# Delta rule and soft mixture of slots on one core: the experts' products turned around and put side by side in the array

## The chip, the cores and the metric

The kernel runs on one core of a Trainium2 chip, in one launch. A core has five engines that work at the same time and wait for each other only through semaphores: TensorE (PE in the profile, with PEld for its loads of the stationary operand), VectorE (DVE), ScalarE (ACT), GpSimd (POOL) and SyncE (SP), which here issues most of the DMAs. The metric is the device time of one execution in microseconds, 921.85 as the median of three (921.1 to 922.2).

A matmul holds one operand still in the 128 x 128 array, at most 128 columns of it, and streams the other one, at most 512 columns here, past it. The result lies in PSUM with one partition for each column of the stationary operand. In float32 each matmul of the program is two MATMUL instructions in the trace, each with a load of its own; a transpose is one.

## The reference, cut to what matters

The first part is a gated delta rule over 768 tokens for 4 batch rows and 8 heads of 48. The change does not touch it. Its output, as x of 3072 tokens by 384, goes through a soft mixture with 8 experts of 4 slots each:

```python
logits = x @ phi                        # 3072 x 32
d = softmax of logits over the tokens   # a column sums to 1
slot_input = (d.T @ x).reshape(8, 4, 384)
for e in range(8):
    h = np.maximum(slot_input[e] @ w1[e], 0.0)    # 4 x 384 @ 384 x 1024
    slot_out[e] = h @ w2[e]                       # 4 x 1024 @ 1024 x 384
c = softmax of logits over the slots    # a row sums to 1
return c @ slot_out.reshape(32, 384)              # 3072 x 32 @ 32 x 384
```

Both w1[e] and w2[e] are 1.57 MB in float32, 25 MB for all experts.

## The kernel before

The first part runs in 24 chunks of 32 tokens, in six groups of four. Each group's logits and both softmaxes (`route`) run beside the next group's chunks, and the slots' sums over the tokens are kept as `sacc`, 96 partitions x 4 x 32: 384 input features (in four pieces `h` of 96) by 32 slots. The token weights over the slots stay in `Call`. The last group's routing has nothing beside it (L529).

The stage of the experts begins at L533, when the buffers of the first part are released (L530). The names that matter:

- `w1t`, `w2t`: an expert's weights on chip. Two w1 (experts 0 and 1) are loaded early in the first part (L499, pool `wpool`); the other 14 tiles, 6 of w1 and 8 of w2, are issued at L534 to L537 on SyncE's queue. A w1 is two DMAs of 48 partitions each, a w2 one DMA of 128 partitions. There are 4 buffers for the later w1 and 5 for w2, so the fifth w1 and the sixth w2 wait until an earlier one was read for the last time.
- L557, `first`: for an expert and each of eight pieces `t` of 128 hidden units, w1's piece (96 x 128) is loaded into the array and the expert's 4 slots stream past it, four times to add up the pieces `h`: 256 matmuls. The result `ph` has the hidden units on partitions, as the second product needs it.
- L561: relu on VectorE, into the expert's own 4 columns of `hx`, whose other columns are zero.
- L568, `second`: `hx` (128 x 32) stands in the array and 384 columns of w2 stream past it, 64 matmuls that all add into one `pso` of 32 partitions x 384.
- L577: 24 transposes make `cT` from `Call`, 32 slots on partitions.
- L582: `so` is `pso` over the softmax's sums. L588: 24 products `pout` of 128 tokens x 384, `cT` standing, `so` streaming, 32 rows deep. L591 and L593 copy each to `ob` on VectorE and ScalarE in turn; L594 stores it from SyncE's queue.

A tile framework orders the instructions of each engine: within its priorities and waits it may put steps of the stage in another order than the code. The order in which TensorE takes them is shown with the change.

Of the kernel before, what the change touches and what calls it, by code (L numbers as in the profile page):

```python
# [16 lines left out]
def kernel(  # L17
# [8 lines left out]
    moe_w2: bass.AP,  # L26
    out: bass.AP,
):
    """Gated delta rule in chunks of 32 tokens, then the slot mixture.

    A "unit" is four heads x 32 tokens of one batch row on the 128 partitions, u = (b, g) with
    head = 4 g + h, partition = 32 h + t.  In a chunk with the state S before it:
        (I + L) w = V - Kn S,   L[t, s] = beta_s kn_t.kn_s  (s < t),   u_s = beta_s w_s
        y = Q S + strict_lower(Q Kn^T) u,      S += Kn^T u
    The inverse of I + L comes from elimination by columns, one 32 x 32 block per partition, for
    four chunks (all their 128 blocks) at once; it doesn't depend on the state and runs ahead.
    The softmax over the tokens is kept online, chunk group by chunk group.
    """
    nc = tc.nc
    P = 128  # L40
    B, H, S, D = q.shape
# [23 lines left out]
    def pt(shape):  # L65
        return ps.tile(shape, F32, name="pt", tag="pt", bufs=2)

# [1 line left out]
    Ks = [io.tile([P, GC, U, DP], F32, name=f"Ks{i}", bufs=1) for i in range(2)]  # L69
    Qs = io.tile([P, GC, U, DP], F32, name="Qs", bufs=1)  # L70
    Vt = {}
# [23 lines left out]
    for i, tag in enumerate(("Lc", "lb", "tt")):  # L95
# [4 lines left out]
                in_=beta.rearrange("b (g h) (c t) -> h (b g) c t", h=4, t=C)[  # L100
                    h, :, i * NB:(i + 1) * NB])
        bts.append(t)
    # the same by blocks: partition 32 h + 8 c + u of a group of chunks
    bb = cpool.tile([P, NG, C], F32, name="bb")
    load_k(0)
    load_q(0, nc.scalar)
# [10 lines left out]
            out=phi[g * D:(g + 1) * D],  # L117
            in_=moe_phi[g * 4 * D:(g + 1) * 4 * D].rearrange("(h d) s -> d h s", h=4))

# [1 line left out]
    ident = cpool.tile([P, P], F32, name="ident")  # L121
    make_identity(nc, ident)
    hm = cpool.tile([P, 4], F32, name="hm")
# [31 lines left out]
        nc.vector.memset(t, 0.0)  # L155
        St.append(t)

# [1 line left out]
    NW1 = 2  # L159
    w1t, w2t = {}, {}  # L160

# [7 lines left out]
    def load_w2(e, pool, bufs):  # L169
        w2t[e] = pool.tile([P, NFC, Dm], F32, name="w2t", tag="w2t", bufs=bufs)  # L170
        nc.sync.dma_start(out=w2t[e], in_=moe_w2[e].rearrange("(t p) d -> p t d", p=P))

# [1 line left out]
    # Each of these gives a list of steps, which the chunks' chain is interleaved with.  # L174
    KQ, AT, KX, Lc, TTb = {}, {}, {}, {}, {}

    def norm(n):
        Kf = Ks[n % 2].rearrange("p c u d -> p (c u) d")
        ssq = small.tile([P, GC * U], F32, name="ssq", tag="ssq")
        nrm = small.tile([P, GC * U], F32, name="nrm", tag="nrm")  # L180
        rn = small.tile([P, GC * U], F32, name="rn", tag="rn")

        def squares():
            sq = wk.tile([P, GC * U, D], F32, name="sq", tag="KX")
            nc.gpsimd.tensor_tensor(sq, Kf[:, :, 0:D], Kf[:, :, 0:D], op=ALU.mult)
            nc.vector.tensor_reduce(ssq, sq, axis=AX.X, op=ALU.add)

        def root():
            # with a Newton step behind the table's value
            nc.vector.tensor_scalar(ssq, ssq, 1e-30, None, op0=ALU.max)  # L190
            nc.scalar.activation(nrm, ssq, ACT.Sqrt)
            nc.vector.reciprocal(rn, nrm)
            nc.vector.tensor_tensor(rn, rn, ssq, op=ALU.mult)
            nc.vector.tensor_tensor(nrm, nrm, rn, op=ALU.add)
            nc.vector.tensor_scalar(nrm, nrm, 0.5, 1e-6, op0=ALU.mult, op1=ALU.add)
            nc.vector.reciprocal(rn, nrm)

        def scale():
            nc.gpsimd.tensor_tensor(Kf[:, :, 0:D], Kf[:, :, 0:D],  # L199
                                    rn.unsqueeze(2).broadcast_to([P, GC * U, D]), op=ALU.mult)  # L200

        return [squares, root, scale]

    def prep(n, c):
        """Of a chunk: Kn and Q transposed, strict_lower(Q Kn^T) and Kn Kn^T (both transposed)."""
        cc = n * GC + c

        def transposes(bh):
# [29 lines left out]
                + [lambda g=g: products(g) for g in range(G)])  # L238

    def invert(n):  # L240
        """(I + L)^-1 transposed: tt[block][k][i] = T[i, k], a block on each partition."""
        st = {}

        def spread():
# [29 lines left out]
        return [spread] + [lambda j=j: eliminate(j) for j in range(C - 1)] + [store]  # L274

    def near(cc):
        """Of the next chunk: its inverse as weights, and Kn spread by heads."""
        n, c = divmod(cc, GC)

        def inverse():  # L280
            for h in range(4):
                nc.sync.dma_start(
                    out=TTs[cc % 2][C * h:C * h + C, :, h, :],
                    in_=TTb[n][C * h + c * U:C * h + (c + 1) * U].rearrange("u k i -> k u i"))

        def keys(g):
            if g == 0:
                KX[cc] = wk.tile([P, G, B, 4, D], F32, name="KX", tag="KX")
            kn = Ks[n % 2].rearrange("p c (b g) d -> p c g b d", g=G)[:, c, g, :, 0:D]
            for b in range(B):  # L290
                nc.gpsimd.tensor_tensor(  # L291
                    KX[cc][:, g, b], kn[:, b].unsqueeze(1).broadcast_to([P, 4, D]),
                    hm.unsqueeze(2).broadcast_to([P, 4, D]), op=ALU.mult)

        return [inverse] + ([lambda g=g: keys(g) for g in range(G)] if cc < NCH - 1 else [])

# [1 line left out]
    def chunk(cc, Yn, fill):  # L298
        n, c = divmod(cc, GC)
        kq, T, at = KQ.pop(cc), TTs[cc % 2], AT.pop(cc)  # L300
# [60 lines left out]
                                 start=False, stop=True, skip_group_check=True)  # L361
            nc.scalar.activation(Yn[:, c, :, g * D:(g + 1) * D], py, ACT.Copy)

# [1 line left out]
    Call = cpool.tile([P, NG, B, NSL], F32, name="Call")  # L365
    dsum = cpool.tile([P, NSL], F32, name="dsum")
    sacc = cpool.tile([GD, 4, NSL], F32, name="sacc")
# [3 lines left out]
    def route(n, Yn):  # L371
# [28 lines left out]
                                    op=ALU.mult)  # L400

        def maximum():
            # the running maximum over the tokens, on every partition
            cm = small.tile([P, NSL], F32, name="cm", tag="cm")
            nc.vector.tensor_reduce(cm, lg.rearrange("p b s -> p s b"), axis=AX.X, op=ALU.max)
            pm = pt([NSL, P])
# [30 lines left out]
                                    op=ALU.mult)  # L437

        def repeat():
            # the weights of 32 tokens, for each of the four heads of a unit  # L440
            pd = pt([P, GC, B, NSL])
            for c in range(GC):
                nc.tensor.matmul(pd[:, c].rearrange("p b s -> p (b s)"),
# [30 lines left out]
    NF = 5  # L474

    class Fill:
        """Some of the steps at each call, evenly over a chunk's NF calls."""

        def __init__(self, steps):
            self.steps, self.at, self.calls = steps, 0, 0  # L480
# [6 lines left out]
                self.steps[self.at - 1]()  # L487

    def merge(*lists):
        """The lists' steps, each list spread evenly over the whole."""  # L490
        keyed = [((i + 0.5) / len(ls), j, f) for j, ls in enumerate(lists) for i, f in enumerate(ls)]
        return [f for _, _, f in sorted(keyed, key=lambda x: x[:2])]

# [35 lines left out]
    drain(routing)  # L529
    att.close()  # L530

# [1 line left out]
    wp2 = ctx.enter_context(tc.tile_pool(name="wts2", bufs=1))  # L533
    for e in range(E):  # L534
        if e >= NW1:
            load_w1(e, wp2, 4)
        load_w2(e, wp2, 5)  # L537
    pd = pt([NSL, 1])
    nc.tensor.matmul(pd, lhsT=dsum, rhs=ones, start=True, stop=True)
    rd = cpool.tile([NSL, 1], F32, name="rd")  # L540
    nc.vector.tensor_scalar(rd, pd, 1e-9, None, op0=ALU.add)
    nc.vector.reciprocal(rd, rd)
    # each expert's slots in their own columns, the others' zero, so that all add up in one place
    hx = wp2.tile([P, E, NFC, NSL], F32, name="hx")
    nc.gpsimd.memset(hx, 0.0)
    pso = ps.tile([NSL, Dm], F32, name="pso", tag="psW")

    def first(e):
        """relu(slots w1), transposed: w1 is the stationary operand."""
        sl = slice(e * SPE, (e + 1) * SPE)  # L550
        st = {}

        def product(t):
            if t == 0:
                st["ph"] = ps.tile([P, NFC, SPE], F32, name="ph", tag="psR", bufs=2)
            for h in range(4):
                nc.tensor.matmul(st["ph"][:, t, :], lhsT=w1t[e][:, h, t * P:(t + 1) * P],  # L557
                                 rhs=sacc[:, h, sl], start=(h == 0), stop=(h == 3))

        def relu():  # L560
            nc.vector.tensor_scalar(hx[:, e, :, sl], st["ph"], 0.0, None, op0=ALU.max)  # L561

        return [lambda t=t: product(t) for t in range(NFC)] + [relu]

    def second(e):
        """w2 is the moving operand, so that its products pass beside the loads of w1."""
        def product(t):
            nc.tensor.matmul(pso, lhsT=hx[:, e, t, :], rhs=w2t[e][:, t, :],  # L568
                             start=(e == 0 and t == 0), stop=(e == E - 1 and t == NFC - 1))

        return [lambda t=t: product(t) for t in range(NFC)]

    cT = wp2.tile([NSL, NG, B, P], F32, name="cT")
    for n in range(NG):
        pc = pt([NSL, B, P])
        for b in range(B):
            nc.tensor.transpose(pc[:, b, :], Call[:, n, b, :], ident)  # L577
        nc.scalar.activation(cT[:, n], pc, ACT.Copy)
    for e in range(E + 1):
        drain(merge(*([second(e - 1)] if e else []), *([first(e)] if e < E else [])))  # L580
    so = cpool.tile([NSL, Dm], F32, name="so")
    nc.vector.tensor_scalar(so, pso, rd, None, op0=ALU.mult)  # L582

    for n in range(NG):
# [38 lines left out]
```

## Time and profile before

| | |
|---|---|
| median of three executions | 921.85 us |
| the profiled execution's span | 919.5 us |
| median less span | 2.35 us |
| span, mean granted clock of TensorE | 0.701 |
| first DMA of the experts' stage issued | at 736.57 us |
| sum `so` begins | at 887.87 us |
| last `pout` product ends | at 915.98 us |

The span runs from the first to the last instruction of the profiled execution. The profile gives each stretch's granted clock of TensorE as a share of 2.4 GHz: 0.50 is its lower level, 1.2 GHz, and 1.00 the upper one. Times in views of the trace count from the start of the span. A busy PE may be streaming, or loading the stationary operand between short streams; the two are told apart by PEld's time beside it.

### The profile page before, as it was taken

Reading aid. Unit: us, or ns where it says so; the run is one execution under the profiler, and the core shown is the slowest. Engines: PE = TensorE matmul, PEld = TensorE weight load, DVE = VectorE, ACT = ScalarE, POOL = GpSimd, SP = SyncE. Lnnn points to the kernel's source line nnn. Section 1 sums busy time; section 2 is a strip of 40 time slices with the busy share of each in tenths; the row PEclk is TensorE's granted clock in tenths of the full one; section 3 lists DMA queues with packets and bytes.
Section 4 is the critical chain, followed back from the end, with each engine's and each line's share of the span. In section 5 each row is a group of like instructions: output and inputs, shape, how many; then the busy total and the mean of one; then the engine's idle time right before and its main releaser. Section 6 shows DMA issues by size and latency. Waiting matters only on the chain.

```text
span 919.5 us, 19108 instructions
## 1 busy us (share of the span) xinstructions
PE 679.9 (74%) x8324; PEld 565.6 (62%) x8324; DVE 299.4 (33%) x816; ACT 101.3 (11%) x223; POOL 192.9 (21%) x347
## 2 busy tenths in 40 slices
PE   1706569069990799807998069996499799999998
PEld 1504569058880688706888058885398696765754
DVE  3267112942139421394213942226421100000011
ACT  0303000021120211102111021111000110000001
POOL 7231213131251213412134111351210200000000
PEclk9999999999995555755557555565555567667765
DMA  6240763023310242102321021000100099990013
GB/s 118 37 85 26 133 115 72 1 52 55 75 20 0 58 70 55 20 0 58 69 55 19 0 58 32 25 2 0 35 13 1 1 266 211 237 231 16 1 60 146
DMA packets 148019, 58.12 MB, mean 63 GB/s; under 512 B 131968, under 2 KB 143328, under 8 KB 147936
## 3 DMA queue, kind: packets, MB, share of 16 engines
q1 hardware_dynamic: 141888, 55.87, 27.9%
q10 hardware_dynamic: 5664, 0.94, 0.6%
q8 instruction: 65, 1.06, 0.5%
q0 software_dynamic: 384, 0.10, 0.1%
q14 instruction: 18, 0.15, 0.1%
HBM read 45.86 MB, written 11.01 MB: 62 GB/s over the span
## 4 chain that ended last, share of the span: by engine, by line
PE 64%; DVE 17%; DMA 6%; POOL 4%; SPq 3%; ACT 3%; issue 2%; ACTq 0%; DVEq 0%; POOLq 0%
PE ph L557 9%; PE psW L324 8%; PE psY L359 7%; DVE pr L264 7%; PE pso L568 6%; PE psS L340 6%; DVE tt L267 6%; PE pt L215 5%; PE pt L385 5%; PE pt L458 3%; PE pout L588 3%; PE psR L310 2%; PE pt L230 2%; PE psY L354 2%; PE pt L379 2%; SPq L77 2%
## 5 line engine op out<-in xcount | busy, mean ns | idle before, releaser
L215 PE MATMUL pt<-ident,Ks 128*128 128x128 f32 x96 | 42.1, 438 | 167.9 <-POOL Ks L199 158.7
L291 POOL TENSOR_TENSOR KX<-Ks,hm 128x192 f32<-128x192 f32 x184 | 91.0, 531 | 354.0 <-PE psS L340 264.4
L215 PEld LDWEIGHTS pt<-ident,Ks 128*128 128x128 f32 x96 | 20.8, 216 | 173.9 <-POOL Ks L199 159.6
L324 PE MATMUL psW<-R,TT 128*128 128x48 f32 x384 | 86.6, 396 | 34.4 <-DMA TT<-td 31.2
L324 PEld LDWEIGHTS psW<-R,TT 128*128 128x128 f32 x384 | 81.1, 311 | 39.4 <-DMA TT<-td 19.1
L557 PEld LDWEIGHTS ph<-sacc,w1t 96*128 96x128 f32 x512 | 87.8, 272 | 3.8 <-issue 3.8
L557 PE MATMUL ph<-sacc,w1t 96*128 96x4 f32 x512 | 88.1, 310 | 0.0
L359 PE MATMUL psY<-U,AT 128*128 128x48 f32 x384 | 83.9, 393 | 0.0
L264 DVE TENSOR_TENSOR pr<-tt,lb 128x31 f32<-128x31 f32 (+15 forms) x186 | 76.7, 413 | 16.2 <-POOL lb L252 11.0
L359 PEld LDWEIGHTS psY<-U,AT 128*128 128x128 f32 x384 | 78.2, 306 | 3.4
L267 DVE TENSOR_TENSOR tt<-tt,pr 128x31 f32<-128x31 f32 (+15 forms) x186 | 73.3, 394 | 5.2
L340 PE MATMUL psS<-U,KX 128*48 128x48 f32 x1472 | 69.8, 271 | 0.0
L340 PEld LDWEIGHTS psS<-U,KX 128*48 128x48 f32 x1472 | 60.8, 181 | 6.3 <-issue 1.7
L568 PE MATMUL pso<-w2t,hx 128*32 128x384 f32 x128 | 58.5, 627 | 1.7 <-DVE hx L561 1.7
L329 DVE TENSOR_TENSOR U<-psW,bta 128x192 f32<-128x192 f32 x48 | 17.2, 358 | 113.4 <-PE psW L324 113.4
L345 DVE TENSOR_TENSOR S<-S,psS 112x384 f32<-112x384 f32 x46 | 25.5, 554 | 87.6 <-PE psS L340 87.3
L233 DVE TENSOR_TENSOR AT<-pt,bdm 128x512 f32<-128x512 f32 x48 | 31.9, 688 | 62.1 <-ACT Lc L232 59.0
L385 PE MATMUL pt<-phi,yT 96*128 96x32 f32 x192 | 45.1, 398 | 6.0 <-ACT yT L381 5.1
L230 PE MATMUL pt<-KQ 48*32 48x64 f32 x1536 | 47.5, 310 | 1.9
L385 PEld LDWEIGHTS pt<-phi,yT 96*128 96x128 f32 x192 | 42.0, 323 | 10.5 <-ACT yT L381 9.1
L561 DVE TENSOR_SCALAR hx<-ph 128x32 f32<-128x32 f32 x8 | 1.5, 192 | 141.0 <-PE ph L557 141.0
L354 PE MATMUL psY<-S,KQ 48*32 48x48 f32 x1536 | 46.1, 265 | 0.1
(107 smaller groups left out, 698.9 us busy)
## 6 DMA issues: line engine op xcount, KB each, us to landing
w1t<-in_moe_w_dram SPq DMA_DIRECT2D x16, 768.0 KB
w2t<-in_moe_w_dram SPq DMA_DIRECT2D x8, 1536.0 KB
Ks<-in_k_dram SPq DMA_DIRECT2D x96, 48.0 KB
V<-in_v_dram SPq DMA_DIRECT2D x96, 48.0 KB
out_dram<-ob SPq DMA_DIRECT2D x24, 192.0 KB
Qs<-in_q_dram SPq DMA_DIRECT2D x80, 48.0 KB
ld<-Lc SPq DMA_DIRECT2D x24, 128.0 KB
lb<-ld SPq DMA_DIRECT2D x6, 512.0 KB
```

The costliest lines, as they stand in the source:

```text
L215: nc.tensor.transpose(tp[:, i, a, :], src[:, c, b * G:(b + 1) * G, :].rearrange("p g d -> p (g d)"), ident)
L230: nc.tensor.matmul(pg[rh, b], lhsT=KQ[cc][r, b, 0, rh], rhs=KQ[cc][r, b, :, rh], start=True, stop=True, skip_group_check=True)
L264: nc.vector.tensor_tensor(prv, tt[:, 0:m, j:j + 1].broadcast_to([P, m, w]), lb[:, j, j + 1:C].unsqueeze(1).broadcast_to([P, m, w]), op=ALU ...
L267: nc.vector.tensor_tensor(tt[:, 0:m, j + 1:C], tt[:, 0:m, j + 1:C], prv, op=ALU.subtract)
L291: nc.gpsimd.tensor_tensor(KX[cc][:, g, b], kn[:, b].unsqueeze(1).broadcast_to([P, 4, D]), hm.unsqueeze(2).broadcast_to([P, 4, D]), op=ALU. ...
L324: nc.tensor.matmul(pw[:, i, g, :], lhsT=T[:, (2 * hf + i) * G + g].rearrange("p h t -> p (h t)"), rhs=Rs[hf][:, i, g, :], start=True, stop ...
L340: nc.tensor.matmul(psS[DP * g:DP * g + D, i, h, :], lhsT=kx[:, g, 2 * hf + i, h, :], rhs=Us[hf][:, i, g, :], start=True, stop=True, skip_g ...
L354: nc.tensor.matmul(py[C * h:C * h + C, b, :], lhsT=kq[r, b, 1, C * h:C * h + C], rhs=old[b // 2][r, b % 2, h, :], start=(b == 0), stop=Fal ...
L359: nc.tensor.matmul(py[:, b, :], lhsT=at[:, g, b].rearrange("p h t -> p (h t)"), rhs=Us[b // 2][:, b % 2, g, :], start=False, stop=True, sk ...
L385: nc.tensor.matmul(pl, lhsT=yT[:, h].rearrange("p c t -> p (c t)"), rhs=phi[:, h, :], start=(h == 0), stop=(h == 3))
L557: nc.tensor.matmul(st["ph"][:, t, :], lhsT=w1t[e][:, h, t * P:(t + 1) * P], rhs=sacc[:, h, sl], start=(h == 0), stop=(h == 3))
L568: nc.tensor.matmul(pso, lhsT=hx[:, e, t, :], rhs=w2t[e][:, t, :], start=(e == 0 and t == 0), stop=(e == E - 1 and t == NFC - 1))
```

## The change

In the experts' stage the roles in the first product are exchanged: all 32 slots (`sacc[:, h, :]`, 96 x 32) stand in the array and 512 columns of w1 stream past. Such a product has 32 result partitions, so four of them, of experts 4 q + 0 to 4 q + 3, are put into the four groups of 32 columns of the array; `ph` is 128 partitions x 512. The hidden units now lie along the free axis, so they are copied with relu to `hr` (ScalarE and VectorE in turn), transposed by TensorE (8 transposes for a set of four experts), and multiplied by a mask `own` that keeps each expert's own 4 of the 32 slots. The second product also runs in the four column groups, with `pso` on 128 partitions, where group j holds the sum over the experts j and 4 + j. `cT` has its 32 rows four times, by 96 plain products instead of 24 transposes, so the last product adds up the four groups: it is 128 rows deep. The sums `rd` are made four times likewise.

The first products of both sets stand ahead of the second products. The loads are issued in another order: w1 of experts 2 to 5, w2 of 0 and 1, w1 of 6 and 7, w2 of 2 to 7. The buffers for w2 are 4 instead of 5.

```diff
-    for e in range(E):
-        if e >= NW1:
-            load_w1(e, wp2, 4)
-        load_w2(e, wp2, 5)
-    pd = pt([NSL, 1])
-    nc.tensor.matmul(pd, lhsT=dsum, rhs=ones, start=True, stop=True)
...
+    for e in range(2, 6):
+        load_w1(e, wp2, 4)
+    for e in range(2):
+        load_w2(e, wp2, 4)
+    for e in range(6, E):
+        load_w1(e, wp2, 4)
+    for e in range(2, E):
+        load_w2(e, wp2, 4)
...
+    own = wp2.tile([P, NQ, 4, NSL], F32, name="own")
+    nc.gpsimd.memset(own, 0.0)
+    for e in range(E):
+        nc.gpsimd.memset(own[:, e // 4, e % 4, e * SPE:(e + 1) * SPE], 1.0)
...
+            for j in range(4):
+                nc.tensor.matmul(pc[NSL * j:NSL * j + NSL, b, :], lhsT=Call[:, n, b, :],
+                                 rhs=ident, start=True, stop=True, skip_group_check=True)
...
-                nc.tensor.matmul(st["ph"][:, t, :], lhsT=w1t[e][:, h, t * P:(t + 1) * P],
-                                 rhs=sacc[:, h, sl], start=(h == 0), stop=(h == 3))
...
+                for j in range(4):
+                    nc.tensor.matmul(ph[NSL * j:NSL * j + NSL], lhsT=sacc[:, h, :],
+                                     rhs=w1t[4 * q_ + j][:, h, f0:f0 + FH],
+                                     start=(h == 0), stop=(h == 3), skip_group_check=True)
+            if f0 == 0:
+                nc.scalar.activation(hr[:, f0:f0 + FH], ph, ACT.Relu)
+            else:
+                nc.vector.tensor_scalar(hr[:, f0:f0 + FH], ph, 0.0, None, op0=ALU.max)
+        for t0 in range(0, NFC, 4):
+            ph = pt([P, 4, P])
+            for t in range(4):
+                nc.tensor.transpose(ph[:, t, :], hr[:, (t0 + t) * P:(t0 + t + 1) * P], ident)
+            nc.vector.tensor_tensor(
+                hT[:, q_, t0:t0 + 4].rearrange("p t j s -> p t (j s)"), ph,
+                own[:, q_].rearrange("p j s -> p (j s)").unsqueeze(1).broadcast_to([P, 4, P]),
+                op=ALU.mult)
+    for q_ in range(NQ):
+        for t in range(NFC):
+            for j in range(4):
+                nc.tensor.matmul(pso[NSL * j:NSL * j + NSL], lhsT=hT[:, q_, t, j, :],
+                                 rhs=w2t[4 * q_ + j][:, t, :],
+                                 start=(q_ == 0 and t == 0), stop=(q_ == NQ - 1 and t == NFC - 1),
+                                 skip_group_check=True)
```

How the instructions stand after this, engine by engine. TensorE before, from the middle of the `cT` transposes (L577) on; L557 is the first product, L568 the second:

```order
L557 MATMUL ph<-sacc,w1t 128x4 x11
L577 MATMUL pt<-ident,Call 32x128 x8
L557 MATMUL ph<-sacc,w1t 128x4 x42
L568 MATMUL pso<-w2t,hx 32x384 x16
L557 MATMUL ph<-sacc,w1t 128x4 x32
L568 MATMUL pso<-w2t,hx 32x384 x8
```

Before, an expert's 32 first products are followed by 8 second products of the expert ahead, and so on to the last. TensorE now, from the products for `cT` (L564) to the last ones (L605); L576 is the first product, L586 the transposes, L594 the second product:

```order
L564 MATMUL pt<-ident,Call 32x128 x96
L576 MATMUL ph<-w1t,sacc 32x512 x32
L586 MATMUL pt<-ident,hr 128x128 x8
L576 MATMUL ph<-w1t,sacc 32x512 x4
L594 MATMUL pso<-w2t,hT 32x384 x2
L576 MATMUL ph<-w1t,sacc 32x512 x28
L586 MATMUL pt<-ident,hr 128x128 x4
L594 MATMUL pso<-w2t,hT 32x384
L586 MATMUL pt<-ident,hr 128x128 x4
L594 MATMUL pso<-w2t,hT 32x384 x61
L605 MATMUL pout<-so,cT 128x384 x24
```

Now all `cT` products come first, then the first set's first products, then the second set's with two early second products among them, and 61 of the 64 second products stand behind both sets. Within a set, the four experts alternate, here in the first half `ph_6958` of the first set (`w1t_631` and `w1t_634` are experts 0 and 1, `w1t_6794` and `w1t_6797` experts 2 and 3):

```order
L576 MATMUL ph_6958<-w1t_6797,sacc_224 32x512
L576 MATMUL ph_6958<-w1t_631,sacc_224 32x512
L576 MATMUL ph_6958<-w1t_634,sacc_224 32x512
L576 MATMUL ph_6958<-w1t_6794,sacc_224 32x512
L576 MATMUL ph_6958<-w1t_6797,sacc_224 32x512
```

So four neighbours in the order go to four column groups, and nothing but their loads must be there. SyncE's queue now, from the first weight of the stage to the stores of the result (L165 is w1, two DMAs each; L171 is w2):

```order
L165 DMA w1t<-in_moe_w_dram 48x4x1024 x8
L171 DMA w2t<-in_moe_w_dram 128x8x384 x2
L165 DMA w1t<-in_moe_w_dram 48x4x1024 x4
L171 DMA w2t<-in_moe_w_dram 128x8x384 x6
L611 DMA out_dram<-ob 128x384 x24
```

Before, two w2 came first and then a w1 and a w2 in turn. The third group here waits for buffers that the first set's first products read, and the last four of the six w2 for buffers that the first set's second products read.

## Rows read from the trace of the kernel before

**Rows 1.** The chain of waits by time; start us, us, what (experts' stage):

```profile
734.99 1.52 PE pt L458 x12
...
764.16 13.05 PE pso L568 x32
...
807.13 6.93 PE pso L568 x16
...
879.61 8.24 PE pso L568 x16
...
887.87 0.62 DVE so L582
...
888.53 27.45 PE pout L588 x48
```

**Rows 2.** Groups by line, 730 to 920 us; busy us, mean ns | idle before:

```profile
L557 PE MATMUL ph<-sacc,w1t 96*128 96x4 f32 x512 | 88.1, 310 | 0.0
L557 PEld LDWEIGHTS ph<-sacc,w1t 96*128 96x128 f32 x512 | 87.8, 272 | 3.8 <-issue 3.8
L568 PE MATMUL pso<-w2t,hx 128*32 128x384 f32 x128 | 58.5, 627 | 1.7 <-DVE hx L561 1.7
L577 PE MATMUL pt<-ident,Call 128*32 128x128 f32 x24 | 4.0, 321 | 0.2 <-DVE rd L541 0.2
```

**Rows 3.** Stretches: PE, PEld, DVE, ACT, POOL busy; PEclk, DMA share, GB/s:

```profile
738.00:746.00 8.00, 8.00 (x58) 7.49 (x58) 0.00 (x0) 2.15 (x5) 0.37 (x1) 0.76 1.02 372
746.00:830.00 84.00, 83.15 (x351) 60.33 (x349) 0.96 (x5) 0.80 (x2) 0.00 (x0) 0.64 1.03 226
830.00:834.00 4.00, 4.00 (x16) 1.58 (x14) 0.00 (x0) 0.00 (x0) 0.00 (x0) 0.90 0.07 26
102.00:120.00 18.00, 7.72 (x188) 7.26 (x184) 3.18 (x8) 0.66 (x2) 3.76 (x8) 1.00 1.04 179
```

**Rows 4.** SyncE's queue by time (start us, us; L171 is w2):

```profile
736.57 1.03 SPq L171 DMA_DIRECT2D w2t<-in_moe_w_dram  x2
```

**Rows 5.** The page: span, a group (mean ns), DMA issues (KB each):

```profile
span 919.5 us, 19108 instructions
...
L233 DVE TENSOR_TENSOR AT<-pt,bdm 128x512 f32<-128x512 f32 x48 | 31.9, 688 | 62.1 <-ACT Lc L232 59.0
...
w1t<-in_moe_w_dram SPq DMA_DIRECT2D x16, 768.0 KB
w2t<-in_moe_w_dram SPq DMA_DIRECT2D x8, 1536.0 KB
```

**Rows 6.** More stretches in the columns of rows 3, for the clock:

```profile
660.00:680.00 20.00, 18.27 (x261) 17.24 (x261) 3.78 (x11) 0.66 (x2) 3.76 (x8) 0.50 0.14 22
734.00:736.00 2.00, 2.00 (x14) 2.00 (x13) 0.56 (x2) 0.00 (x0) 1.72 (x5) 0.68 0.00 0
764.00:768.00 4.00, 4.00 (x8) 1.20 (x9) 0.19 (x1) 0.00 (x0) 0.00 (x0) 0.50 1.02 189
770.00:778.00 8.00, 8.00 (x31) 3.12 (x29) 0.00 (x0) 0.00 (x0) 0.00 (x0) 1.00 1.07 240
889.00:892.00 3.00, 3.00 (x11) 1.76 (x10) 1.12 (x2) 0.98 (x2) 0.00 (x0) 1.00 0.32 121
894.00:916.00 22.00, 21.96 (x35) 10.99 (x33) 4.46 (x8) 4.42 (x9) 0.00 (x0) 0.50 0.41 152
```

**Rows 7.** ScalarE's copies of every second result tile, by time (start us, us):

```profile
889.48 0.49 ACT L593 ACTIVATE ob<-pout 128x384 f32<-128x384 f32 x1 [142.41 <-PE pout L588]
890.76 0.49 ACT L593 ACTIVATE ob<-pout 128x384 f32<-128x384 f32 x1 [0.80 <-PE pout L588]
...
909.60 0.49 ACT L593 ACTIVATE ob<-pout 128x384 f32<-128x384 f32 x1 [2.07 <-PE pout L588]
912.16 0.49 ACT L593 ACTIVATE ob<-pout 128x384 f32<-128x384 f32 x1 [2.07 <-PE pout L588]
```

**Rows 8.** A chunk's products in column groups, by time (start us, us):

```profile
665.52 1.52 PE L340 MATMUL psS<-U,KX 128*48 128x48 f32 x32
...
672.01 0.60 PE L310 MATMUL psR<-S,KQ 48*32 48x48 f32 x32
```

## What the change does to the time: a prediction made before it ran

> **What bounds the kernel now.** I read the chain of waits first. From 737 us on it is TensorE alone: first products, second products by turns, then `so` at 887.87 and 27.45 us of `pout` to 915.98 [rows 1]. Then the groups by line. The first products keep TensorE busy 88.1 us, and the loads of their standing operand 87.8 us: four streamed columns hide nothing, so this stage is bound by loading w1 into the array, 512 times 128 columns [rows 2]. The second products stream: 58.5 us for 128 instructions [rows 2]. Together 147 us.
>
> Then the stretches of the DMAs beside it. They are full from 738 to 830 us (share 1.02 and 1.03) and still trickle at 26 GB/s to 834 [rows 3]. So the last weights are there some 54 us before TensorE has done with them; that is what a faster TensorE can at most win before the transfers decide, and how they come in matters then. The 372 GB/s from 738 to 746 are the two w2 issued first at 736.57 [rows 3, 4]; the 179 GB/s from 102 to 120 are the two early w1 with little beside them [rows 3]. Each tile is 1.57 MB [rows 5]: 4.2 us for a w2, 8.8 us for a w1. Eight of one and six of the other make 87 us, where the trace needs 92 (738 to 830); putting all that lacks on w1 makes 9.7. I take 9.2, and the trickle of 4 us as a delay that a long queue builds up.
>
> Last the clock. L588 shows what a streamed product costs at each level: ScalarE takes every second tile, 1.28 us apart at clock 1.00 and 2.56 apart at 0.50 [rows 6, 7]. A tile is two instructions of 384 columns, hence 320 ns each at the upper and 640 at the lower level; for 512 columns 427 and 853.
>
> **Do column groups overlap?** The chunks have it already. At clock 0.50 [rows 6] 48 columns cost 80 ns by the same measure; 32 instructions in two column groups at L340 are 2.56 us one by one and take 1.52, and 32 at L310, in four groups and two halves of rows, take 0.60, over four at once [rows 8]. Not shown are four groups with 96 or 128 rows and 512 columns each. The ends are 853 ns an instruction (no overlap) and 213 (all four); I take four, since L310 is the nearest row.
>
> The Trainium skill, "TensorE: Matmul & The Clock Gate", Part 3, measured 2.38 times for three column groups at 512 columns, so less than the number of groups. By 3.2 of four the sum below would be some 5 us longer; the row at L310 shows no such loss, though with short streams.
>
> **The new course, step by step, on the span's time.** SyncE issues w1 of experts 2 to 5, two w2, two w1, two w2, and then four w2 into buffers that the first set's second products read. First bytes come at 738, as before: the last wait is again for the end of the last routing.
> 1. Experts 2 to 5's w1: 4 x 9.2, to 774.8. Two w2: 783.3. Two w1: 801.7; with 3 us of the trickle they have landed at 804.7. Two w2 land at 813.2.
> 2. The first set has its last w1 at 756.4. Behind it stand 26 products, 52 instructions, four at once 13 x 853 = 11.1 us: done by 768, so the buffers for the sixth and seventh w1 come free 15 us before the queue reaches them. The 96 `cT` products (192 instructions of 213 ns at the lower level, 10 us in four groups; at the ends 41 and 5) lie in the wait from 737 to 756, as do `own` and `rd`. At 41 us they would end at 778, still ahead of 804.7; there is cover. In the first set relu, eight transposes and the mask (688 ns for such a tile on VectorE, L233 [rows 5]) are hidden in the wait for 804.7 too.
> 3. Second set, first products: 26 behind the last w1, 11.1 us at the lower level. TensorE has waited before, so it starts low. The 16-instruction bursts at L568 are the same case: 16 x 640 = 10.2 us, but 6.93 to 8.24 were taken [rows 1], as the clock rises inside (0.50 in 764 to 768, 1.00 in 770 to 778 [rows 6]). I take off 2.7: 8.4 us, to 813.1. Relu (0.7, as L233) and four transposes add 1.3: 814.4; the two w2 have landed by then.
> 4. Second products of the first set: 29 left, 58 instructions, 14.5 x 320 = 4.6 us, to 819.0. Only now are four w2 buffers free, and the transfers have run dry since 813. Issue to first bytes is 1.4 us (736.57 to 738), then 4 x 4.2, 1 us of trickle: 838.3. This is a wait that the change adds: SyncE's queue holds nothing else then but the stores at the end, so only TensorE waits.
> 5. Second set's second products: 29 behind the last w2, 14.5 x 640 = 9.3 us, less 2.7 again: 844.9. `so` and its step 0.7: 845.6.
> 6. `pout`: 24 tiles. Before, it lost the upper level by 894 with 32 rows streaming [rows 6]. Now 128 rows stream. L568 gained it with 128 rows and 32 columns, and L458, 128 rows by 96 columns, gained it in 734 to 736 [rows 1, 6]. So I let it stay high: 24 x 0.64 = 15.4, to 861.0. The ends are 15.4 and 30.7. Copies (0.49 on ScalarE) keep up, as they did at 889 to 892 [rows 7].
> 7. Last copy, store and end: 919.5 - 915.98 = 3.5 us. Span 864.5.
>
> The span before was 919.5 [rows 5], the median 2.35 us more, so 867 us against 921.85. Of the 55 us, some 43 come from the products no longer ending the stage (`so` at 845 instead of 888), 12 from the clock in `pout`. What is late next is the last four w2.
>
> **Rivals.**
> - *The clock falls in `pout` as before.* The busy PE of 894 to 916 at 0.50 speaks for it, the 32 rows against it. 27.45 instead of 15.4: 879.
> - *TensorE stays at the lower level in all of the stage.* It now works in bursts between transfers. Step 3 is 11.1, step 4 9.3, step 5 9.3, `pout` 30.7: 2.7 + 4.7 + 2.7 + 15.3 more, 892. The bursts at L568 rise in time, which speaks against it; but those had no idle TensorE before them.
>   The Trainium skill, "TensorE: Matmul & The Clock Gate", "Loop structure matters more than you think", says this of loops that wait for a transfer between bursts: they run at the lower level. By that rule 892; the trace before has no such wait in this stage.
> - *The groups overlap less.* With the upper level and none at all, step 3 is 22.2 + 2.7, step 4 18.6, step 5 18.6 + 2.7, in all 45 us more: 912. With pairs 15 us more: 882. The 0.60 us at L310 speak against it, its short streams of 48 rows do not settle it.
> - *Slower: no overlap and the lower level.* Then the first set's 52 instructions take 44.4 us, the sixth w1 starts late (802 instead of 783), the last w1 lands at 822.8, and steps 3 to 5 cost 44.4, 37.1 and 37.1 us: 1000. One mechanism decides: at the lower level the three bursts are 118.6 us divided by the overlap; at an overlap of two the time is 922, below that it is slower than before.
>
> **How the numbers follow.** My forecast 867, 0.60. `pout` low 879, 0.12. All low 892, 0.10. Less overlap with the clock rising (882 to 912) 0.11. No overlap, low (over 922) 0.05. A course of the transfers that I do not see 0.02, at no change. The range: at the bottom w1 at 8.8 instead of 9.2 (2.4 us), no trickle (4), bursts 4 us shorter, 1 more for w2 at a higher rate, near 855; at the top the case of all low, 893. This leaves out about 0.15. Differences under 0.2% cannot be told from none. Faster 0.93, within 0.2% 0.02, slower 0.05.
>
> **What would show it.** The first products' group should fall from 88 us to some 20, with little idle issue inside a burst and PEld far below PE; four neighbours should start within some tens of ns. The DMA share should have a hole of a few us near 815 to 820 and end near 838. The chain should name the w2 before the last second products and, ahead of it, w1. PEclk should be 1.00 in `pout`, and its tiles 0.64 us apart. I am wrong if first products start 400 or 800 ns apart, if `pout` tiles are 1.28 us apart, or if the last w1 lands much later than 805.

## The result, and the profile after

The changed kernel takes 862.75 us (median of four, 861.4 to 863.78), the kernel before 921.48 in the runs beside it: a ratio of 0.9372, 95% interval 0.9353 to 0.9390. The forecast was 867, with 855 to 893 as its range. The profiled execution, the shortest of the four, has a span of 859.7 us and a time of 861.4.

The page first: span, the engines' busy time, and what the DMAs moved in 40 slices.

```profile
span 859.7 us, 18725 instructions
PE 577.3 (67%) x8130; PEld 470.3 (55%) x8130; DVE 301.9 (35%) x814; ACT 102.8 (12%) x225; POOL 191.7 (22%) x355
GB/s 118 27 112 2 101 142 109 18 21 61 80 38 16 0 72 71 51 21 1 56 45 94 20 2 32 32 58 1 2 0 43 9 2 0 138 203 244 182 261 220
```

The last row of the kernel before:

```profile
GB/s 118 37 85 26 133 115 72 1 52 55 75 20 0 58 70 55 20 0 58 69 55 19 0 58 32 25 2 0 35 13 1 1 266 211 237 231 16 1 60 146
```

TensorE has lost about a hundred us of busy time (679.9 before), and the DMA row no longer has two nearly empty slices before the stores (16 and 1 GB/s before): the stage now runs mostly at the pace of the transfers. The groups of the experts' stage by line (busy us, mean ns of one | idle before, releaser) answer to [rows 2]:

```profile
L576 PE MATMUL ph<-w1t,sacc 96*32 96x512 f32 x128 | 32.6, 774 | 25.4 <-DMA w1t<-in_moe_w_dram 25.4
L594 PE MATMUL pso<-w2t,hT 128*32 128x384 f32 x128 | 20.8, 586 | 17.2 <-DMA w2t<-in_moe_w_dram 17.2
L605 PE MATMUL pout<-so,cT 128*128 128x384 f32 x48 | 15.7, 488 | 0.7 <-DVE so L599 0.7
L564 PE MATMUL pt<-ident,Call 128*32 128x128 f32 x192 | 5.7, 274 | 0.2 <-DVE sacc L464 0.2
```

The first products fell from 88.1 to 32.6 us, the second from 58.5 to 20.8, and both now wait for loads, 42.6 us in all. `mean ns of one` is no price here: 128 times 774 ns would be 99 us, and the group was busy for 32.6, so several run at once.

The chain of waits in the same stage, in order of time (start us, us, what), answers to [rows 1]:

```profile
735.89 20.03 DMA w1t<-in_moe_w_dram
...
756.05 9.18 PE ph L576 x52
...
774.48 22.95 DMA w1t<-in_moe_w_dram
...
797.57 8.89 PE ph L576 x52
...
808.39 5.29 PE pso L594 x58
813.68 0.38 SPq L171
...
816.45 14.79 DMA w2t<-in_moe_w_dram
...
831.29 7.41 PE pso L594 x58
...
838.73 0.63 DVE so L599
...
839.40 6.08 PE pout L605 x18
```

Before, nearly every link of it was TensorE. Now two loads of w1 and one of w2 carry 58 us (each from its issue to its landing, with what was queued ahead of it), and TensorE stands between them with three bursts and behind them with a fourth. The stretches (columns as in [rows 3]) show the transfers and the clock:

```profile
736.00:754.00 18.00, 9.77 (x168) 4.77 (x160) 0.00 (x0) 3.58 (x6) 0.00 (x0) 0.80 1.03 184
754.00:770.00 16.00, 12.24 (x64) 3.72 (x64) 1.98 (x3) 0.60 (x1) 0.00 (x0) 0.80 1.03 175
773.00:779.00 6.00, 4.70 (x6) 0.54 (x5) 0.00 (x0) 0.00 (x0) 0.00 (x0) 0.63 1.07 403
782.00:796.00 14.00, 4.77 (x6) 0.53 (x4) 0.00 (x0) 0.00 (x0) 0.00 (x0) 0.50 1.02 195
804.00:806.00 2.00, 2.00 (x12) 0.44 (x4) 0.00 (x0) 0.00 (x0) 0.00 (x0) 1.00 0.04 14
806.00:813.00 7.00, 7.00 (x69) 2.91 (x68) 2.04 (x3) 0.00 (x0) 0.00 (x0) 1.00 0.00 0
814.00:816.00 2.00, 0.00 (x0) 0.00 (x0) 0.00 (x0) 0.00 (x0) 0.00 (x0) 1.00 0.75 207
816.00:830.00 14.00, 4.43 (x6) 0.54 (x6) 0.00 (x0) 0.00 (x0) 0.00 (x0) 0.59 1.06 401
842.00:856.00 14.00, 13.14 (x41) 7.41 (x39) 6.02 (x11) 5.04 (x11) 0.00 (x0) 1.00 0.77 289
```

w1 moves at 175 to 195 GB/s, w2 at 401 to 403, and from 804 until past 813 next to nothing moves: the hole. In `pout` (842 to 856) the clock stays at 1.00, where it was 0.50 before [rows 6].

### The profile page after: what moved, and what is told of

It reads as the page before. It is cut to its first block, busy times and chain, and to the rows that moved or that the text cites. A ratio compares the mean times of both kernels' runs of the same rounds, so it can differ in the third digit from the quotient of the medians.

```text
span 859.7 us, 18725 instructions
## 1 busy us (share of the span) xinstructions
PE 577.3 (67%) x8130; PEld 470.3 (55%) x8130; DVE 301.9 (35%) x814; ACT 102.8 (12%) x225; POOL 191.7 (22%) x355
## 4 chain that ended last, share of the span: by engine, by line
PE 55%; DVE 19%; DMA 13%; POOL 4%; SPq 3%; ACT 3%; issue 2%; ACTq 0%; DVEq 0%; POOLq 0%
PE psW L324 9%; PE psY L359 9%; DVE pr L264 7%; PE psS L340 7%; DVE tt L267 6%; PE pt L215 5%; DMA w1t<-in_moe_w_dram 5%; PE pt L385 5%; PE pt L458 4%; PE psR L310 3%; PE psY L354 3%; PE pt L230 3%; DMA TT<-td 2%; PE pt L379 2%; PE ph L576 2%
## 5 line engine op out<-in xcount | busy, mean ns | idle before, releaser
L576 PE MATMUL ph<-w1t,sacc 96*32 96x512 f32 x128 | 32.6, 774 | 25.4 <-DMA w1t<-in_moe_w_dram 25.4
L362 ACT ACTIVATE Y<-psY 128x192 f32<-128x192 f32 x48 | 15.9, 331 | 252.5 <-PE psY L359 252.5
L230 PEld LDWEIGHTS pt<-KQ 48*32 48x32 f32 x1536 | 34.4, 155 | 14.7 <-ACT KQ L218 11.7
L453 POOL TENSOR_TENSOR db<-dr,hm 128x128 f32<-128x128 f32 x96 | 36.1, 414 | 21.4 <-ACT dr L448 20.3
```

The lines of the kernel that those rows point to most:

```text
L230: nc.tensor.matmul(pg[rh, b], lhsT=KQ[cc][r, b, 0, rh], rhs=KQ[cc][r, b, :, rh], start=True, stop=True, skip_group_check=True)
L453: nc.gpsimd.tensor_tensor(db[:, b], st["dr"][:, c, b].unsqueeze(1).broadcast_to([P, 4, NSL]), hm.unsqueeze(2).broadcast_to([P, 4, NSL]), o ...
L576: nc.tensor.matmul(ph[NSL * j:NSL * j + NSL], lhsT=sacc[:, h, :], rhs=w1t[4 * q_ + j][:, h, f0:f0 + FH], start=(h == 0), stop=(h == 3), sk ...
```

## The experiments

All were timed beside the kernel before on the same chip; it took 921.23 us beside e1 to e4, 919.20 beside e5 to e8 and 919.21 beside e9 and e10, so medians of different groups compare to within some 2 us. Times are medians; "after" stands for 862.75.

**e1: one column group instead of four.** Of the first products, only the piece `h = 0` keeps its own group:

```diff
-                    nc.tensor.matmul(ph[NSL * j:NSL * j + NSL], lhsT=sacc[:, h, :],
+                    g0 = NSL * (j if h == 0 else 0)
+                    nc.tensor.matmul(ph[g0:g0 + NSL], lhsT=sacc[:, h, :],
```

> The changed kernel, with the first products for the feature pieces h = 1 to 3 of all four experts of a set sent to column group 0 instead of each to its own; this leaves those pieces out of three experts' sums. Theory (the overlap of the four groups made the first products short): behind the last w1 stand 2 products in their own groups and 24 in one, 48 instructions one after another, at 427 ns (upper level) some 20.5 us and 2 to 3 more until the clock has risen, 23 instead of the 8.9 us that the profile after shows; the first set's burst becomes as long but ends at about 779 us, still before the sixth w1 could start; so about 14 us longer than 862.75, 877 us. Rival (the transfers hide TensorE, overlapping or not): 863 us. Rival (without overlap the clock stays at the lower level): 41 us instead of 8.9 in the second set, and the sixth w1 some 17 us late: about 905 to 912 us.

Measured: 876.41 us, ratio 0.9524 (0.9493 to 0.9556), 13.7 more than after. TensorE in time order (start us, us), with the clock of the middle of the burst from a stretch:

```profile
797.34 22.76 PE L577 MATMUL ph<-w1t,sacc 96*32 96x512 f32 x52 [4.70 <-DMA w1t<-in_moe_w_dram]
```
```profile
800.00:818.00 18.00, 18.00 (x44) 4.58 (x43) 0.00 (x0) 0.60 (x1) 0.00 (x0) 0.96 0.25 93
```

The same 52 instructions take 22.76 us instead of 8.89. So the overlap is real with 96 rows and 512 columns. With most of the first products one after another the kernel still beats the one before; the clock rose in the burst (0.96). The prediction's slower rival needed the lower level and no overlap in the second products either, and neither occurred here.

**e2: no hole.** The second products of a set follow its first ones, and the loads come in that order:

```diff
-    for e in range(2, 6):
+    for e in range(2, 4):
         load_w1(e, wp2, 4)
-    for e in range(2):
+    for e in range(4):
         load_w2(e, wp2, 4)
-    for e in range(6, E):
+    for e in range(4, E):
         load_w1(e, wp2, 4)
-    for e in range(2, E):
+    for e in range(4, E):
         load_w2(e, wp2, 4)
...
-    for q_ in range(NQ):
         for t in range(NFC):
             for j in range(4):
```

> The changed kernel with the second products of a set right behind its first ones, and the loads in the order w1 of 2 and 3, w2 of 0 to 3, w1 of 4 to 7, w2 of 4 to 7, so that the last four w2 buffers come free at about 778 us, long before the queue gets to them. Theory (the last four w2 waited for buffers, and that hole of the transfers sits on the path): the last w2 lands some 8 us earlier, 855 us. Rival (the transfers are bound by what comes after or by their own rate, a hole shifts nothing): 863 us.

Measured: 855.79 us, 0.9300 (0.9270 to 0.9331); 7.0 less than after, 8 expected. In the chain (start us, us) SyncE's own issuing stands ahead of the last load, and no product any more; the transfers are full from 740 to 820 (a share of 1.00 to 1.10 in stretches of 4 us):

```profile
803.84 6.46 SPq L171
...
810.39 14.86 DMA w2t<-in_moe_w_dram
...
825.30 7.06 PE pso L593 x58
```

From the first weight's issue (737.36 there, 734.50 after) to the last landing it is 87.9 us instead of 96.7. The wait that step 4 named was on the path, and worth 7 us of the time.

**e3: `pout` 32 rows deep again.**

```diff
-            nc.tensor.matmul(po, lhsT=cT[:, n, b, :], rhs=so, start=True, stop=True)
+            nc.tensor.matmul(po, lhsT=cT[0:NSL, n, b, :], rhs=so[0:NSL], start=True, stop=True)
```

> The changed kernel with pout only 32 rows deep (rows 0 to 31 of cT and of so), as before; this leaves three of the four partial sums out of the result. Theory (128 streaming rows kept the clock at its upper level in pout): the clock falls a few us into pout as in the profile before, tiles 1.28 us apart from there, 862.75 + 10 to 12 = 873 to 875 us. Rival (the dense bursts ahead of pout, or the stage as a whole, keep it high): 863 us.

Measured: 875.28 us, 0.9508 (0.9483 to 0.9534), 12.5 more than after. ScalarE's copies by time and two stretches:

```profile
843.22 0.49 ACT L610 ACTIVATE ob<-pout 128x384 f32<-128x384 f32 x1 [36.70 <-PE pout L605]
844.51 0.49 ACT L610 ACTIVATE ob<-pout 128x384 f32<-128x384 f32 x1 [0.80 <-PE pout L605]
846.30 0.49 ACT L610 ACTIVATE ob<-pout 128x384 f32<-128x384 f32 x1 [1.29 <-PE pout L605]
848.86 0.49 ACT L610 ACTIVATE ob<-pout 128x384 f32<-128x384 f32 x1 [2.07 <-PE pout L605]
```
```profile
839.00:843.00 4.00, 3.29 (x28) 1.18 (x21) 0.62 (x1) 0.00 (x0) 0.00 (x0) 1.00 0.01 4
850.00:870.00 20.00, 20.00 (x33) 10.19 (x31) 4.46 (x8) 3.93 (x8) 0.00 (x0) 0.50 0.42 158
```

The copies go from 1.29 to 2.56 us apart and the clock from 1.00 to 0.50, with TensorE busy without a gap: the picture of [rows 6, 7] again.

**e4: the kernel before with `pout` 128 rows deep**, rows 32 to 127 zero on both sides:

```diff
-    cT = wp2.tile([NSL, NG, B, P], F32, name="cT")
+    cT = wp2.tile([P, NG, B, P], F32, name="cT")
+    nc.gpsimd.memset(cT[NSL:2 * NSL], 0.0)
+    nc.gpsimd.memset(cT[2 * NSL:P], 0.0)
...
+    so = cpool.tile([P, Dm], F32, name="so")
+    nc.gpsimd.memset(so[NSL:2 * NSL], 0.0)
+    nc.gpsimd.memset(so[2 * NSL:P], 0.0)
+    nc.vector.tensor_scalar(so[0:NSL], pso, rd, None, op0=ALU.mult)
```

> The kernel before with pout 128 rows deep, rows 32 to 127 of cT and so being zeros, nothing else changed and nothing left out. Theory (the streaming rows alone keep the clock up): pout takes 15.7 us instead of 27.4 and the time is 910 us. Rival (rows of zeros do not count, or the change's other parts held the clock): 921.5 us, no change.

Measured: 912.27 us, 0.9900 (0.9863 to 0.9937): 9 less than before (6 to 13 by the interval), 11 expected. The profiled execution was the shortest of the four, 907.2 us where the others took 911.8 to 913.0. In it the clock is at the upper level to the end of `pout`, and rows of zeros are enough for it:

```profile
888.00:892.00 4.00, 4.00 (x14) 2.35 (x13) 1.62 (x3) 1.48 (x3) 0.00 (x0) 1.00 0.80 298
892.00:904.00 12.00, 8.80 (x28) 4.88 (x26) 4.46 (x8) 3.44 (x7) 0.00 (x0) 1.00 0.75 279
```

So some 9 to 12 us of the gain (e4 and e3) has nothing to do with the experts' products: it comes from the four copies of the slots' rows in `cT`.

**e5: w1's halves on two queues**, on top of e2:

```diff
-            nc.sync.dma_start(
+            (nc.scalar if g and e > 1 else nc.sync).dma_start(
                 out=w1t[e][g * D:(g + 1) * D],
```

> The kernel of e2 (second products behind each set's first, no hole), with the upper half of each later w1 (partitions 48 to 95) issued from ScalarE's queue instead of SyncE's, so that both halves of a w1 move at the same time. In the profile after, six w1 take 9.1 us each back to back and a w2 of the same size 4.1. Theory (a DMA that goes to only 48 partitions can't use the whole rate; two such at once complement each other): a w1 in 5.5 to 7 us, six of them 12 to 20 us less, 836 to 844 us against e2's 855.8. Rival (w1's rows or packets are slow whatever goes beside them): 856 us. Rival (ScalarE's queue holds up cT and relu behind its DMA issues): 858 us or more.

Measured: 850.81 us, 0.9252 (0.9230 to 0.9275), between the two: the interval just touches that of e2, and the 12 us expected at least did not come. The edit moved more than the loads. ScalarE by time (idle before, releaser): after two of six `cT` copies it waits 20 us for TensorE, on which the framework now has most of the `cT` products behind the wait for the first set's last w1.

```profile
758.84 0.60 ACT L566 ACTIVATE cT<-pt 128x512 f32<-128x512 f32 x1 [19.95 <-PE pt L564]
```

So ScalarE did not hold up TensorE, against the third rival, but the order changed on both. In the stretch of the later w1 the transfers were no faster, 155 GB/s from 780 to 804 where e2 has 190 from 784 to 806; but w2 and single halves are mixed in differently, so whether two halves at once move faster stays open.

**e6: the last four w2 in halves**, on top of e2:

```diff
-    for e in range(4, E):
-        load_w2(e, wp2, 4)
+    for e in range(4, E):
+        w2t[e] = wp2.tile([P, NFC, Dm], F32, name="w2t", tag="w2t", bufs=4)
+    for t0 in range(0, NFC, 4):
+        for e in range(4, E):
+            nc.sync.dma_start(out=w2t[e][:, t0:t0 + 4],
+                              in_=moe_w2[e].rearrange("(t p) d -> p t d", p=P)[:, t0:t0 + 4])
```

> The kernel of e2, with the last four w2 loaded in two pieces each, first the hidden pieces t = 0 to 3 of all four experts, then t = 4 to 7. Theory (the burst behind the last landing is on the path and its length is what stands behind the last wait): 13 products instead of 29 are left there, 3.5 to 4 us instead of 7.0, so 852 to 853 us against e2's 855.8. Rival (smaller DMAs cost as much in landing as the shorter burst gives): 856 us.

Measured: 852.56 us, 0.9265 (0.9223 to 0.9307), 3.2 less than e2 in the medians, though the intervals overlap. Part of that may be the group it was timed in; the profiles show the mechanism. The burst behind the last landing is shorter still than expected, 2.78 us where e2 has 7.06 (chain, start us, us):

```profile
814.13 11.18 DMA w2t<-in_moe_w_dram
825.36 2.78 PE pso L597 x26
```

**e7: 8 buffers for the result tiles** (`bufs=8` for `ob`), on top of e6.

> The kernel of e6 with 8 buffers instead of 4 for the result tiles. In the profile after, copies wait for stores from 846 us on, eight times, but the last product ends 15.75 us after the first began. Theory (pout is bound by TensorE's 0.64 us a tile, the waits for stores take up slack): within 1 us of e6. Rival (the stores pace the end of the kernel): 1 to 2 us less than e6.

Measured: 851.32 us, 0.9257 (0.9232 to 0.9282): 1.2 less than e6 in the medians, which would suit the rival, but the intervals overlap, and these times cannot tell the two apart. The traces can. The last copy (start us, us), first in e6, where the last product ends at 844.58, then in e7, where it ends at 844.82:

```profile
844.80 0.56 DVE L611 COPY ob<-pout 128x384 f32<-128x384 f32 x1 [0.40 <-DMA out_dram<-ob]
```
```profile
844.86 0.56 DVE L611 COPY ob<-pout 128x384 f32<-128x384 f32 x1 [0.73 <-PE pout L608]
```

In e7 no copy waits for a store any more, and the last one begins 0.04 us after the last product instead of 0.22. The waits were slack but for 0.2 us.

**e8: w1 in rows of 2 KB**, on top of e2:

```diff
-            nc.sync.dma_start(
-                out=w1t[e][g * D:(g + 1) * D],
-                in_=moe_w1[e, g * 4 * D:(g + 1) * 4 * D].rearrange("(h d) f -> d h f", h=4))
+            for f0 in ((0,) if e < 2 else (0, F // 2)):
+                f1 = F if e < 2 else f0 + F // 2
+                nc.sync.dma_start(
+                    out=w1t[e][g * D:(g + 1) * D, :, f0:f1],
...
```

> The kernel of e2 with each later w1 half in two DMAs of half the hidden units, rows of 2 KB instead of 4 KB. Theory (the number of partitions that a DMA reaches sets its rate): w1 stays at about 9 us, 856 us. Rival (the length of the rows sets it): w1 at 5 to 7 us, 836 to 848 us, or at more than 9 us and above 858.

Measured: 849.39 us, 0.9238 (0.9206 to 0.9270), 6.4 less than e2 in the medians, with intervals that just touch, and a little short of the 836 to 848 that the rival gave. TensorE by time shows what it was: from the burst that the last w2 of the first four released to the one that the last w1 released. First e2, then e8:

```profile
776.45 8.14 PE L593 MATMUL pso<-w2t,hT 128*32 128x384 f32 x58 [5.75 <-DMA w2t<-in_moe_w_dram]
...
810.14 10.06 PE L576 MATMUL ph<-w1t,sacc 96*32 96x512 f32 x52 [3.65 <-DMA w1t<-in_moe_w_dram]
```
```profile
773.86 7.50 PE L595 MATMUL pso<-w2t,hT 128*32 128x384 f32 x57 [5.92 <-DMA w2t<-in_moe_w_dram]
...
800.81 9.70 PE L578 MATMUL ph<-w1t,sacc 96*32 96x512 f32 x52 [2.86 <-DMA w1t<-in_moe_w_dram]
```

Four w1 in 33.7 us, and in 27.0: 8.4 and 6.7 us each (e9 below has 7.6 with the same rows). Whether the shorter row or the finer turn-taking of the two halves did it, e8 can't say, since both changed. The theory that the number of partitions alone sets the rate is wrong.

**e9: e6 and e8 together**, and **e10: the same with rows of 1 KB.**

> The kernel of e6 (no hole, last w2 in halves) with the w1 rows of 2 KB of e8. Theory (the two gains are in different stretches: e8's in the rate of w1, e6's in the burst behind the last landing): both add, 846 us (e8's 849.4 less 3). Rival (the earlier end of the loads is lost again, since the last first products then decide): 849 us.

> As e9 with w1 rows of 1 KB, in four DMAs for each half. Theory (e8 gained since more DMAs to different partitions lie in the queue at once, or since shorter packets share a target better): w1 again faster than in e9, 840 to 844 us. Rival (it is used up at 2 KB, or issuing 48 DMAs costs as much): 846 to 850 us.

Measured: e9 845.8 us, 0.9197 (0.9164 to 0.9230), as the sum of the two gains had it. e10 844.49, 0.9187 (0.9167 to 0.9207): not to be told from e9, so no further gain of 1 KB rows is shown. These two beat the changed kernel by 17 and 18 us, some 2 of which may be the group they were timed in. The two bursts of e8 again, in e9:

```profile
772.85 7.87 PE L599 MATMUL pso<-w2t,hT 128*32 128x384 f32 x57 [5.27 <-DMA w2t<-in_moe_w_dram]
...
803.40 9.97 PE L582 MATMUL ph<-w1t,sacc 96*32 96x512 f32 x52 [3.17 <-DMA w1t<-in_moe_w_dram]
```

Four w1 take 30.6 us here, 29.8 in e10 (774.27 to 804.02), and 34.3 in e6 with its rows of 4 KB (775.87 to 810.17). So the cut took some 10 to 20% off a w1, and the 6.7 us of e8 did not come again.

## Why the prediction was right

Runs of the same first part differ by some us in when the stage begins (first weight's issue at 736.57 before, 734.50 after, 737.36 in e2), so the steps are compared from there. The stage took 182.9 us before; forecast 127.9 (736.57 to 864.5); measured 125.2 (734.50 to 859.7). Of the 4.8 us by which the span came out below the forecast, 2.1 are the earlier beginning, which the prediction did not treat.

1. *Loads to the last w1: 68.1 us forecast, 62.9 measured* (797.44). The course was as said. The terms were too large: the 3 us of trickle, for which nothing is left in the chain, and the tiles. From the first bytes at 735.89 it is 61.5 us; less two w2 of 3.9 (1.57 MB at 403 GB/s), where 4.2 were taken, six w1 have 9.0 each as a mean, where 9.2 were taken.
2. *The first set's burst and `cT` hidden: yes, with the spare that was said.* The burst ended at 765.23, and SyncE got to the sixth w1 at 766.30, not at 783, since it issues ahead of the transfers. But the transfers had room: in e1 this burst ended at 778.65, 13.4 us later, SyncE issued the sixth w1 only at 777.83, and the last w1 released its burst at 797.34, where after has 797.57. SyncE's queue after, then e1's first burst and its queue, by time (start us, us):

```profile
766.30 9.11 SPq L165 DMA_DIRECT2D w1t<-in_moe_w_dram  x4
```
```profile
755.41 23.24 PE L577 MATMUL ph<-w1t,sacc 96*32 96x512 f32 x52 [4.97 <-DMA w1t<-in_moe_w_dram]
777.83 1.88 SPq L165 DMA_DIRECT2D w1t<-in_moe_w_dram  x4
```

   `cT` took 5.7 us, the lower of its bounds within a us: four groups at the upper level (1.00 from 734 to 742).
3. *Second set's first burst: 8.4 forecast, 8.89 measured, by two errors of opposite sign.* The forecast divided 52 instructions by four, 13 steps. But the expert whose w1 lands last has all its eight products left, 16 instructions for one column group, so there are 16 steps: twelve of four instructions and four of one. Short windows of TensorE's order near the end of the burst (start us, us) show them:

```profile
804.15 0.64 PE L576 MATMUL ph<-w1t,sacc 96*32 96x512 f32 x4
804.58 0.59 PE L576 MATMUL ph<-w1t,sacc 96*32 96x512 f32 x1
805.01 0.59 PE L576 MATMUL ph<-w1t,sacc 96*32 96x512 f32 x1
```

   A step is 0.43 us, whether it holds four instructions or one. At the lower level 16 steps of 853 ns would be 13.6 us; the rise of the clock (0.50 from 796 to 800, 1.00 from 802) took 4.8 off, where 2.7 were taken. That the two nearly cancel is luck. e1 shows that it is the overlap which makes the burst short: 13.7 us in the time, 14 expected.
4. *First set's second products: 4.6 forecast, 5.29 measured, then 19.3 and 17.6 to the last landing.* The hole came earlier and was longer than said: the transfers ran dry at 804, not at 813, and began again at about 814; e2 takes it out for 7 us. The four groups overlapped in full, as I took it, and what was mis-sized is again the count: 16 steps instead of 14.5, the last two of them single instructions. 16 of 0.32 us are 5.2.

```profile
812.54 0.51 PE L594 MATMUL pso<-w2t,hT 128*32 128x384 f32 x4
812.86 0.49 PE L594 MATMUL pso<-w2t,hT 128*32 128x384 f32 x1
```

   The Trainium skill, "TensorE: Matmul & The Clock Gate", Part 3, measured 2.38 for three groups; the steps of this trace show no such loss. Relu and transposes ahead of it took 1.9 instead of 1.3.
5. *Last burst: 6.6 forecast, 7.41 measured.* 16 steps again instead of 14.5, 10.2 us at the lower level, and the rise of the clock took 2.8 off. The bursts did start at the lower level after each wait (0.50 from 754 to 760, 796 to 800 and 822 to 834) and rise inside, as those of [rows 1, 6]. The Trainium skill's rule in "Loop structure matters more than you think" of the same page holds for their start alone; the case of all low (892) did not come.
6. *`pout`: 15.4 forecast, 15.75 measured, at 1.00 throughout.* Shown from both sides: 32 rows in the new kernel lose it (12.5 us), 128 rows in the old one keep it (9 us).
7. *Tail: 3.5 forecast, 4.6 measured.* The last copy waited for a store and began 0.4 us after the last product. That is the smaller part: in e7 no copy waits, and the tail is 4.5 us all the same. What makes the rest stays open.

The differences partly cancel: 5.2 less at 1, 1.7 less in the loads of 4, some 4 more in the bursts and the end. So the course, the waits, the overlap and the clock in `pout` were as said, and the sizes were good to a few us each, but for the count of steps in a burst; that the stage's sum was off by only 2.7 is better than its terms. Two of the signs named came otherwise: the hole lay from 804 to 814 instead of 815 to 820, and the first products' group took 32.6 us instead of some 20. The two bursts are 18.1 of these; the rest are products of one expert at a time, in the waits, where they cost nothing.

The forecast split the 55 us as 43 from the products and 12 from the clock in `pout`. The runs give 9 to 12 for the latter, and e1 gives 14 for the overlap of the first products. No run takes the rest apart into the swapped operands and the overlap of the second products.

## What to carry to other kernels

Where a few columns stream past a loaded operand, compare the two groups by line, the matmuls and their loads: if both are busy alike, as here with 88.1 and 87.8 us, the stage pays for loading the array, and here turning the operands and filling the column groups removed that. Then price the stage that is left by its transfers: which order they come in, which buffer each waits for, and how much work stands behind the last landing; here e2, e6 and e8 together (e9) found some 16 us there. The work behind a landing is at least what the last tile itself feeds to its one column group, 16 steps here, and e6 halved that. And read the granted clock beside the depth of a product: making a shallow streaming product deeper, with zeros if need be, was worth 9 us by itself.

## What the runs showed that I had not expected

- The rate of w1 follows how it is cut: 8.4 to 8.6 us a tile with rows of 4 KB (e2, e6), 6.7 and 7.6 with 2 KB in twice as many DMAs (e8, e9), 7.4 at 1 KB (e10); a w2 of the same size takes 3.9 at 401 GB/s. Why w1 is slower is not shown.
- Four column groups overlapped in full: a step of four instructions took as long as one instruction, 0.43 us for 512 columns and 0.32 for 384 at the upper level.
- Rows of zeros held the clock as well as data did (e4).
